# Gated mix of a long convolution and a mixer layer on one core: two row repairs of the filter fold done by VectorE, with another order of all instructions

## The chip, the cores and the metric

The kernel runs on one core of a Trainium2 chip. The metric is the device time of one execution in microseconds; shown are the median of several runs and one profiled execution. A core has five instruction queues that run side by side and meet only at semaphores: TensorE (PE, matmuls), VectorE (DVE), ScalarE (ACT), GpSimd (POOL) and SyncE (SP, which here only issues DMAs).

## The reference

The input x has 2048 rows of 640 bf16 values. Two branches are computed from it and mixed with a gate for each row.

```
g = sigmoid((x * gate_w).sum(-1))
a = x * (y + kv * ssm_D)        # kv = (k convolved with 4 taps) * v
                                # y  = long causal convolution of kv with ssm_k over 2048 rows, by FFT
h  = gelu(layernorm(x) @ w1)    # 640 -> 640, then its four quarters are shifted by 1, -1, 2, -2 rows
x1 = x + shifted(h) @ w2
b  = x1 + gelu(layernorm(x1) @ w3) @ w4     # 640 -> 1536 -> 640
out = g * a + (1 - g) * b
```

## The kernel before, in words

The rows form 16 tiles of 128 rows; the 640 channels form 5 chunks of 128.

**The mixer branch.** ln1 (L846) takes mean and variance of a tile with batch-norm instructions on VectorE, the reciprocal root (rstd) with one POOL instruction (L811), normalises on VectorE (L858) and transposes on TensorE (pe_turn, L839). mm1 (L863) multiplies by w1 and ScalarE applies gelu on the way out of PSUM. mm2 (L895) multiplies by w2 and adds the result to x on VectorE (L909, which also gives the row sums). ln2 (L916) normalises again: for tiles 0 to 7 on VectorE with a DMA transpose by SP (ln_apply, L825), for the others on ScalarE. mm3 (L930) and mm4 (L952) are the two large products, in four blocks of 512 rows.

**The convolution branch.** A transform of 2048 points is made of small matmuls with constant matrices, after rows have been added and subtracted in pairs ("folds") so that fewer products are needed. The filter's chunk c goes through three functions. h_load (L729) loads it. h_fold (L732) adds ssm_D, makes sums and differences of rows and their mirror on VectorE (L737, L738), copies the 16 unpaired elements (L739), and lets SP transpose the result into tile T (L740). A second fold (L721) then makes sums and differences of T into tile U. Two rows don't fit the pattern and are repaired on partition 0: in T a run of 4 x 128 elements is copied to another place of T (L743), and 8 x 128 elements of U overwrite elements of T (L744). h_chunk (L746) multiplies T and U with the constant Rh: its first four products read U (L749, L750), the other four read T (L751, L752) and so need the repairs. ScalarE copies each result out of PSUM into the filter's transform HF. The two pairs T, U alternate between chunks, so the fold of chunk c + 2 waits for the products of chunk c. The signal goes the same way: kv_load (L755) transposes k and v on loading, kv_fold (L762) makes the four taps, the product with v and the folds, x_fwd (L784) multiplies into XF. Later, unit (L972) multiplies the transforms on VectorE, with some sums made by accumulating DMAs from POOL (L987), and final (L1011) transforms back, applies the gate and either adds to the output in memory with an accumulating POOL DMA (L1036, for the first 12 of 16 units) or writes it by SP (L1039).

**What sets the order.** The program records 1200 operations in the order of the calls (L1054 to L1115). The list SEQUENCE holds their numbers in the order in which they are issued; each engine takes its own operations from that list, in order, and never overtakes. The numbers are those of recording, so number 410 is the same operation in any list. PLACES gives each of the 213 PSUM tiles its bank. schedule (L255) adds the dependence of a tile on the copying out of the tile that held its banks before, and emit (L276) turns the dependences that are left into semaphore waits. A DMA's place in the list is its place in the queue of its engine: the transfers of SP and the DMAs, rstd and gate instructions of POOL each wait in line.

Operations that the prediction names: 404, the second sum of the last filter fold (L724); 410, its first product on that sum (L750); 457, the normalising of tile 3 in ln2 (L826), whose transpose is 458; the first mm3 group (L934), which is 505 in the list before; 45, the load of Rh (L675); 349, h_load of chunk 2 (L730).

Of the kernel before, what the change touches and what calls it, by code (L numbers as in the profile page):

```python
# [414 lines left out]
def bass_gated_mix__ssm_conv_h3__mixer_s_mlp__prompt_kernel(  # L415
# [32 lines left out]
    def ps(n, cls):  # L448
# [3 lines left out]
    SEQUENCE = [40, 58, 0, 6, 2, 7, 5, 38, 41, 8, 59, 43, 3, 4, 1, 9, 39, 60, 10, 61, 11, 12, 46, 42, 13, 141, 14, 142, 15, 62,  # L452
# [463 lines left out]
    def ln2(t):  # L916
        ln_math(1, t)
        x, xn, mean, rstd = X[:, t, :], xnb[t % 3], st[1, 2][:, t:t + 1], st[1, 5][:, t:t + 1]
        if t < LNA:
            ln_apply(1, t, mean, x, xn, chunk_of[1, t // 4], ALU.add)  # L920
            return
# [226 lines left out]
```

## Time and profile before

| | |
|---|---|
| median of 3 runs | 234.4 us (234.22 to 234.96) |
| the profiled execution, whole | 233.44 us |
| its span, first to last instruction | 231.6 us |
| granted TensorE clock, mean | 0.990 |
| busy: PE, DVE, ACT, POOL | 215.5, 209.1, 187.2, 75.5 us |
| DMA packets, moved | 74258, 42.68 MB |

A line of the page's groups reads: line of the code, engine, operation, output and input with shape, count, then busy time, mean time of one in ns, and the idle time of the engine just before it with what ended it. "L615", "L620" and "L625" are the helpers through which nearly all VectorE and ScalarE instructions are recorded, "L635" the helper of the matmuls, "L238" of the DMAs. PSall is PSUM; arena is the one SBUF tensor that holds every tile. SPq and POOLq are DMA issues. Matmuls overlap in the records, so busy time divided by count is the better measure of what one costs.

### The profile page before, as it was taken

The numbers are of one execution on the slowest core, as the hardware profiler recorded it, in microseconds if no ns is written. First come the engines' busy times: TensorE is split into PE (matmuls) and PEld (weight loads), VectorE is DVE, ScalarE is ACT, GpSimd is POOL, SyncE is SP. The second block draws the span as 40 slices with busy tenths as digits, with TensorE's granted clock in tenths as the row PEclk, the third lists the DMA queues.
The fourth block names the chain that finished last, engine by engine and source line by source line (L and its number), as shares of the span: only waits on it lengthen the run. The fifth ranks groups of instructions, "written<-read, shape, count | busy, mean of one in ns | idle before, by whom it ended". The sixth has DMA issues, their size and how long they took to land.

```text
span 231.6 us, 3931 instructions
## 1 busy us (share of the span) xinstructions
PE 215.5 (93%) x1455; PEld 127.5 (55%) x1455; DVE 209.1 (90%) x362; ACT 187.2 (81%) x352; POOL 75.5 (33%) x86
## 2 busy tenths in 40 slices
PE   6989899999999987999999999999999999999940
PEld 2678555674554542445765456744677545777720
DVE  5997899998989969899969999998899999899890
ACT  2389979999999999999937999759998778436960
POOL 1313020244124030240344233442234352648851
PEclk9999999999999999999999999999999999999996
DMA  5999969997877997697798499699989999799994
GB/s 175 372 259 292 236 96 231 186 273 150 173 205 158 146 272 166 137 327 109 178 200 136 97 198 182 141 171 179 294 155 203 193 164 149 116 174 124 109 161 84
DMA packets 74258, 42.68 MB, mean 184 GB/s; under 512 B 54266, under 2 KB 69503, under 8 KB 74239
## 3 DMA queue, kind: packets, MB, share of 16 engines
q1 hardware_dynamic: 64912, 30.55, 55.1%
q0 software_dynamic: 9152, 11.82, 34.2%
q8 instruction: 11, 0.18, 0.3%
q10 hardware_dynamic: 174, 0.07, 0.2%
q14 instruction: 9, 0.07, 0.1%
HBM read 14.88 MB, written 6.55 MB: 93 GB/s over the span
## 4 chain that ended last, share of the span: by engine, by line
PE 64%; ACT 19%; DVE 6%; issue 3%; DMA 3%; POOL 2%; POOLq 1%
PE PSall L635 60%; ACT arena L625 19%; DVE arena L615 3%; PE PSall L658 3%; DMA arena<-arena 3%; POOL out_dram L238 2%; DVE arena L620 1%; PE PSall L841 1%; DVE arena L909 1%; POOLq L1118 1%; POOL arena L811 0%; DVE arena L655 0%; PE PSall L690 0%; DVE arena L645 0%; DVE arena L662 0%
## 5 line engine op out<-in xcount | busy, mean ns | idle before, releaser
L635 PE MATMUL PSall<-arena 128*128 128x320 bf16 (+4 forms) x1341 | 204.0, 310 | 5.9 <-ACT arena L625 3.4
L615 DVE TENSOR_TENSOR arena<-arena 128x320 bf16<-128x320 bf16 (+6 forms) x201 | 163.4, 862 | 6.7 <-ACT arena L625 3.1
L635 PEld LDWEIGHTS PSall<-arena 128*128 128x128 bf16 x1341 | 120.1, 98 | 88.9 <-ACT arena L625 14.5
L625 ACT ACTIVATE arena<-PSall 128x512 bf16<-128x512 f32 (+8 forms) x187 | 107.6, 626 | 19.0 <-PE PSall L635 13.7
L625 ACT ACTIVATE arena<-arena 128x1 f32<-128x1 f32 (+5 forms) x115 | 69.3, 645 | 6.6 <-POOL arena L811 3.4
L238 POOL DMA_DIRECT2D arena<-arena x22 | 20.5, 954 | 68.5 <-DVE arena L615 56.5
L238 POOL DMA_DIRECT2D out_dram<-arena x28 | 30.5, 1192 | 30.5 <-ACT arena L625 23.6
L811 POOL TENSOR_TENSOR arena<-arena 128x1 f32<-128x1 f32 (+1 forms) x26 | 23.0, 898 | 40.2 <-DVE arena L620 40.1
L625 ACT ACTIVATE arena<-PSall,arena 128x640 bf16<-128x640 f32 (+1 forms) x32 | 20.3, 657 | 10.0 <-PE PSall L635 9.4
L620 DVE TENSOR_SCALAR arena<-arena 128x640 bf16<-128x640 bf16 (+4 forms) x65 | 22.5, 367 | 3.1 <-ACT arena L625 2.2
L909 DVE SCALAR_TENSOR_TENSOR arena<-PSall,arena 128x640 bf16<-128x640 f32 x16 | 13.1, 820 | 4.3 <-PE PSall L635 4.1
L807 DVE BATCH_NORM_STATS2 arena<-arena 128x6 f32<-128x320 bf16 x32 | 14.2, 477 | 1.5 <-DMA arena<-in_A_q_dram 1.5
L658 PE MATMUL PSall<-arena 128*128 128x512 bf16 x28 | 8.4, 446 | 2.1 <-DVE arena L655 2.1
L841 PE MATMUL PSall<-arena 128*128 128x128 bf16 x80 | 6.7, 219 | 0.4 <-ACT arena L625 0.2
L658 PEld LDWEIGHTS PSall<-arena 128*128 128x128 bf16 x28 | 3.0, 112 | 5.6 <-DVE arena L655 2.1
L841 PEld LDWEIGHTS PSall<-arena 128*128 128x128 bf16 x80 | 5.0, 97 | 1.2 <-ACT arena L625 0.6
L620 POOL TENSOR_SCALAR arena<-arena 128x16 f32<-128x16 f32 x3 | 1.9, 635 | 10.8 <-ACT arena L625 10.0
L625 ACT ACTIVATION_READ_ACCUMULATOR arena<-arena 128x1 f32 x16 | 3.3, 208 | 0.0
L808 DVE BATCH_NORM_AGGREGATE arena<-arena 128x2 f32<-128x12 f32 x16 | 2.9, 197 | 0.1
L664 ACT ACT_TABLE_LOAD x1 | 1.3, 1283 | 2.1 <-issue 2.1
L615 POOL TENSOR_TENSOR arena<-arena 128x16 f32<-128x16 f32 x3 | 2.6, 869 | 0.7 <-DVE arena L620 0.5
L909 DVE DVE_READ_ACCUMULATOR arena<-PSall,arena 128x1 f32 x16 | 1.3, 82 | 0.0
(19 smaller groups left out, 3.4 us busy)
## 6 DMA issues: line engine op xcount, KB each, us to landing
arena<-arena POOLq DMA_DIRECT2D x12, 640.0 KB, 6.5
arena<-in_A_q_dram SPq DMA_DIRECT2D x14, 320.0 KB, 5.3
out_dram<-arena POOLq DMA_DIRECT2D x20, 160.0 KB, 4.4
arena<-in_A_ssm_k_dram SPq DMA_DIRECT2D x5, 512.0 KB, 4.7
arena<-in_B_w_dram SPq DMA_DIRECT2D x1, 1920.0 KB, 8.6
out_dram<-arena SPq DMA_DIRECT2D x10, 160.0 KB, 2.7
arena<-in_B_w_dram SPq DMA_DIRECT2D x1, 1152.0 KB, 5.5
out_dram<-arena SPq DMA_DIRECT2D x12, 80.0 KB, 2.7
```

Of the source, the lines that this page charges most:

```text
L238: fn = lambda e: e.dma_start(out, in_, **kw)
L615: P.op(eng, lambda e: e.tensor_tensor(o, real(a), real(b), op), [a, b], [o], dve_ns(o, [a, b], 2) if eng == "dve" else 500)
L620: P.op(eng, lambda e: e.tensor_scalar(o, real(a), s1, s2, op0=op0, **({} if op1 is None else {"op1": op1})), [a] + aps, [o], dve_ns(o, [a] ...
L625: P.op("act", lambda e: e.activation(real(o), real(a), f, bias=bias, scale=scale, **({"accum_out": accum} if accum is not None else {})), ...
L635: fns.append(lambda e, l=l, r=r, i=i: e.matmul(real(o), l, r, start=(i == 0), stop=(i == last)))
L658: P.op("pe", lambda e: e.matmul(real(pw), warm[:, 0:128], warm[:, 128:640], start=True, stop=True), [warm], [pw], 427.0)
L807: P.op("dve", lambda e, o=o, i=i: e.bn_stats(o, i), [i], [o], 400)
L808: P.op("dve", lambda e: e.bn_aggr(bna[:, t, :], bns[k]), [bns[k]], [bna[:, t, :]], 120)
L811: P.op("pool", lambda g: g.tensor_tensor(o, a, e, ALU.pow), [a, e], [o], dur)
L841: P.op("pe", [lambda e, c=c, pb=pb, xn=xn: e.transpose(real(pb)[:, 128 * c:128 * (c + 1)], xn[:, 128 * c:128 * (c + 1)], ident) for c in r ...
L909: P.op("dve", lambda e: e.scalar_tensor_tensor(x, real(pr), 1.0, x, op0=ALU.mult, op1=ALU.add, accum_out=st[1, 0][:, t:t + 1]), [pr, x], [ ...
L1118: with nc.Block() as block:
```

## The change

The two repairs of each chunk's fold, ten in all, are made by a VectorE tensor_scalar (times 1.0) on one partition instead of POOL DMAs. SEQUENCE and PLACES are new throughout: each operation keeps its number, the ten repairs move from POOL's queue to VectorE's, and the order on all five engines and the banks of most PSUM tiles are others. A branch in ln2 is added that PT2 = () leaves unused.

```
-    SEQUENCE = [40, 58, 0, 6, 2, 7, 5, 38, 41, 8, 59, 43, 3, 4, 1, 9, 39, 60, 10, 61, 11, 12, 46, 42, 13, 141, 14, 142, 15, 62,
...
+    SEQUENCE = [40, 58, 3, 1, 38, 8, 41, 59, 7, 6, 5, 9, 42, 4, 2, 0, 39, 60, 10, 11, 61, 12, 46, 13, 43, 141, 14, 15, 142, 16,
...
-    PLACES = [0, 1, 4, 2, 5, 0, 0, 1, 2, 3, 4, 5, 3, 2, 5, 6, 3, 5, 7, 3, 3, 0, 5, 4, 6, 1, 7, 0, 6, 3, 7, 3, 4, 4, 2, 3, 2, 2,
...
+    PLACES = [0, 1, 1, 2, 6, 5, 3, 2, 3, 4, 5, 6, 7, 6, 7, 1, 4, 1, 0, 7, 5, 1, 6, 6, 3, 2, 0, 5, 5, 2, 4, 5, 0, 7, 6, 0, 6, 6,
...
-        P.dma("pool", T5[0:1, :, 1, 1], T5[0:1, :, 0, 0])
-        P.dma("pool", T[0:1].rearrange("p (i e n) -> p i e n", e=2, n=128)[:, :, 0], U[0:1].rearrange("p (i e n) -> p i e n", e=2, n=128)[:, :, 1])
+        for o, a in ((T5[0:1, :, 1, 1], T5[0:1, :, 0, 0]),
+                     (T[0:1].rearrange("p (i e n) -> p i e n", e=2, n=128)[:, :, 0], U[0:1].rearrange("p (i e n) -> p i e n", e=2, n=128)[:, :, 1])):
+            if ROWFIX:
+                ts(o, a, 1.0, None, ALU.mult)
+            else:
+                P.dma("pool", o, a)
...
+    ROWFIX = 1
...
+        if t < LNA and t in PT2:
+            ts(xn, x, mean, rstd, ALU.add, ALU.mult)
+            pe_turn(t, xn, chunk_of[1, t // 4])
+            return
```

Where the places that the prediction names stand in the two lists (the numbers of the operations left and right of a mark; "..." leaves out what lies between):

```
before: ... 403 678 ... 404 ... 614 ... 753 ... 602 ... 410 411 ... 413 ... 505
after:  ... 404 ... 403 410 411 ... 405 ... 406 ... 753 ... 413 ... 457 ... 602 ... 511
before, SP: 202 (x), 327 (h_load 1), ... 349 (h_load 2), 310 (transpose, fold 0), 526 (v), 45 (Rh), 552 (k, chunk 1)
after,  SP: 202, 327, 305, ... 310, 552, 526, 349, 251 (x), 45
```

In the new list the first mm3 group is 511; between 410 and it stand three mm2 tiles (731, 732, 676, 677, 753, 754) and the products of chunk 4 and of x_fwd chunk 2.

138 rows, old and new, of tables (PLACES, SEQUENCE) are left out of this document.

## The prediction

> **What bounds the kernel now.** I read first the page's busy shares, then the windows by stage, then the timelines and the chain of waits in the one stage where TensorE stands still.
>
> ```profile
> span 231.6 us, 3931 instructions
> PE 215.5 (93%) x1455; PEld 127.5 (55%) x1455; DVE 209.1 (90%) x362; ACT 187.2 (81%) x352; POOL 75.5 (33%) x86
> ...
> 10.00:30.00 20.00, 18.07 (x223) 14.40 (x222) 18.00 (x56) 18.22 (x45) 3.61 (x5) 1.00 1.08 258
> 50.00:80.00 30.00, 29.07 (x206) 15.69 (x204) 28.27 (x57) 29.86 (x61) 7.62 (x10) 1.00 0.83 174
> 80.00:90.00 10.00, 7.89 (x42) 3.71 (x41) 7.74 (x15) 10.00 (x11) 2.27 (x4) 1.00 1.03 262
> 90.00:100.00 10.00, 9.75 (x46) 4.16 (x45) 9.11 (x12) 9.97 (x20) 1.47 (x2) 1.00 0.64 158
> 100.00:220.00 120.00, 120.00 (x750) 72.57 (x749) 113.55 (x136) 94.62 (x177) 49.07 (x47) 1.00 0.91 169
> ```
>
> The columns behind the stretch are its length, then PE, PEld, DVE, ACT and POOL busy, and the clock. From 100 to 220 us TensorE is busy 120.00 of 120.00 us at clock 1.00: nothing that feeds it there is worth anything unless it becomes late. What is to be had lies before. The idle time of PE is 1.93 us from 10 to 30, 0.93 from 50 to 80, and 2.11 + 0.25 = 2.36 from 80 to 100: 5.2 us at most. The stretch from 80 to 92 is where the last chunk of the filter fold and its repairs stand. VectorE is nearly as full as TensorE (28.27 of 30 us from 50 to 80), and the change gives it more to do.
>
> ```profile
> 75.66 6.59 PE L635 MATMUL PSall<-arena 128*128 128x512 bf16 x37
> 83.17 3.69 PE L635 MATMUL PSall<-arena 128*128 128x320 bf16 x20 [0.93 <-DVE arena L909]
> 87.88 1.04 PE L635 MATMUL PSall<-arena 128*128 128x512 bf16 x4 [1.01 <-ACT arena L625]
> 89.08 1.89 PE L635 MATMUL PSall<-arena 128*128 128x512 bf16 x8 [0.17 <-DMA arena<-arena]
> 91.22 1.04 PE L635 MATMUL PSall<-arena 128*128 128x512 bf16 x4 [0.25 <-ACT arena L625]
> ```
> ```profile
> 82.64 6.30 DMA arena<-arena
> ```
>
> The chain of waits (start, length, what) runs through the second repair of chunk 4: issued at 82.64, landed at 88.94, and the products that need it start at 89.08. But the timeline of PE beside it shows that the landing itself costs 0.17 us. The waits ahead of it are for L909 on VectorE (0.93) and for PSUM banks that ScalarE had not copied out (1.01 and 0.25). So a faster repair alone gives 0.17 us; the rest must come from the order.
>
> **The change, part by part.**
>
> *Ten transfers go.* Ten POOL DMAs (L743, L744) leave POOL and the queue.
>
> ```profile
> L238 POOL DMA_DIRECT2D arena<-arena x22 | 20.5, 954 | 68.5 <-DVE arena L615 56.5 <-DMA arena<-arena 12.0
> arena<-arena POOLq DMA_DIRECT2D x5, 1.0 KB, 2.3
> arena<-arena POOLq DMA_DIRECT2D x5, 2.0 KB, 3.4
> ```
>
> At 954 ns a DMA, POOL loses 9.5 us of 75.5 us busy; it is busy 33% of the span, so this is worth nothing by itself. What matters is POOL's queue: it stood 56.5 us behind the folds' VectorE instructions (L615), with rstd for later tiles queued behind. In the new order rstd and gate come right after each other. No row shows that a TensorE group waited for rstd, so I count nothing. The latency of 2.3 and 3.4 us goes from all five chunks; only chunk 4's is on the path (0.17 us).
>
> *Ten copies come to VectorE*, on one partition, 512 and 1024 elements. The trace has no copy on one partition of this length. The nearest rows:
>
> ```profile
> L679 DVE TENSOR_SCALAR arena<-arena 128x640 bf16<-128x640 bf16 x1 | 0.3, 272 | 0.0
> L620 DVE TENSOR_SCALAR arena<-arena 128x2048 bf16<-128x2048 bf16 x10 | 7.5, 745 | 0.1
> L620 DVE TENSOR_SCALAR arena<-arena 128x16 bf16<-128x16 bf16 x5 | 1.0, 202 | 0.1
> L655 DVE MEMSET arena<- 128x640 bf16 x1 | 0.6, 592 | 0.1
> ```
>
> The line through 640 elements (272 ns) and 2048 (745 ns) has 0.336 ns an element: 229 and 401 ns, five of each 3.15 us. From below, ten at the 202 ns of the 16-element form: 2.0 us. From above, the memset's 592/640 = 0.925 ns an element: 474 and 947 ns, 7.1 us. I take 3.15, since L679 is the same operation on the same type at nearly this length. The Trainium skill, "VectorE: DVE Perf Modes", section "The TRN2 errata", gives 58 cycles plus elements/4 at 0.96 GHz whatever the partitions; an estimate by that page is 194 and 327 ns, 2.6 us for the ten. The 272 ns row is above that page's 227 ns, so the row goes into the sum.
>
> *The new order at the end of the head.* The numbers of SEQUENCE are operations in the order of recording, so the two lists can be lined up. Three steps matter.
>
> First, chunk 4's products on U (op 410, L750), which started at 87.88. Of the work ahead of it on PE, three mm2 tiles (30 matmuls of 320 columns) and fourteen matmuls of 512 columns now stand behind it.
>
> ```profile
> L635 PE MATMUL PSall<-arena 128*128 128x320 bf16 x696 | 100.3, 299 | 3.2 <-ACT arena L625 1.2 <-DVE arena L615 1.1 <-DVE arena L909 0.9
> L635 PE MATMUL PSall<-arena 128*128 128x512 bf16 x420 | 96.1, 379 | 1.6 <-ACT arena L625 1.3 <-DMA arena<-arena 0.2
> 79.70 0.68 DVE L615 TENSOR_TENSOR arena<-arena 128x1024 bf16<-128x1024 bf16 x1
> 82.28 0.82 DVE L909 SCALAR_TENSOR_TENSOR arena<-PSall,arena 128x640 bf16<-128x640 f32 x1 [0.99 <-PE PSall L635]
> 83.03 0.44 DVE L620 TENSOR_SCALAR arena<-arena 128x640 bf16<-128x640 bf16 x1
> 84.74 0.82 DVE L909 SCALAR_TENSOR_TENSOR arena<-PSall,arena 128x640 bf16<-128x640 f32 x1 [1.27 <-PE PSall L635]
> ```
>
> Busy over count is 0.144 and 0.229 us, so PE has 30 x 0.144 + 14 x 0.229 = 7.5 us less to do first. It would be there at 87.88 - 1.01 - 0.93 - 7.5 = 78.4. It needs the fold's second sum (op 404), which ended at 79.70 + 0.68 = 80.4. Ahead of that, VectorE now has eight of the copies (4 x 0.63 = 2.5 us) and one small instruction (0.2), and no longer has one 1024-element sum, two L909, one 640-element and one small instruction (0.68 + 1.64 + 0.44 + 0.2 = 3.0): it ends 0.3 us sooner, at 80.1. So PE now waits 1.7 us there, for VectorE instead of ScalarE and the DMA. The two waits of VectorE for PE (0.99 and 1.27) should shrink, as the products that it waited for now come ahead of the instructions that read them.
>
> Second, the entry into mm3, from which PE does not stop again. Between op 410 and the first mm3 group lie 30 matmuls of 320 and 22 of 512 columns, 4.3 + 5.0 = 9.4 us: it starts at 80.1 + 9.4 = 89.5. Before, it started at 91.22 with four 512-column matmuls (0.9 us) more behind it, which is 90.3 in the new count. Gain 0.8 us. The condition is that tile 3's normalised rows have arrived.
>
> ```profile
> 76.66 1.20 SPq L235 DMA_TRANSPOSE arena<-arena  x1
> arena<-arena SPq DMA_TRANSPOSE x26, 3.7
> ```
>
> They left VectorE (op 457) for this transfer at 76.6. Op 457 now has more VectorE work ahead: ten copies 3.15, five 1024-element sums 3.4, one 2048-element scaling 0.75, two L909 1.64 and three small ones 0.84 are 9.8 us, less the 0.07 us by which each of the 21 overlaps the next (82.28 + 0.82 against the next start at 83.03), 8.3 us. It ends at 84.9, and 3.7 us later, at 88.6, mm3 can start: 0.9 us to spare.
>
> Third, SyncE. The constant of the filter transform (op 45) goes behind a transposed load of 3.88 us and two plain loads, h_load 2 (op 349) behind the same.
>
> ```profile
> 25.49 0.58 SPq L238 DMA_DIRECT2D arena<-cRh  x1
> 26.11 3.88 SPq L235 DMA_TRANSPOSE arena<-in_A_k_dram  x1
> 34.67 3.55 PE L635 MATMUL PSall<-arena 128*128 128x512 bf16 x15
> arena<-cRh SPq DMA_DIRECT2D x1, 448.0 KB, 4.6
> arena<-in_A_ssm_k_dram SPq DMA_DIRECT2D x5, 512.0 KB, 4.7
> ```
>
> The constant is issued at about 25.49 + 3.88 + 1.0 = 30.4 and lands at 35.0; its first product starts ten 512-column matmuls into the group at 34.67, near 36.8. Cost nothing, cover 1.8 us. h_load 2 leaves near 29.3 and lands at 34.0, for a VectorE instruction at 34.5: cover 0.5 us, and beyond it each microsecond is VectorE's and then PE's.
>
> *Other moves.* The 0.25 us at 91.22 was a bank: fewer banks are behind in the new list, since the chunk 4 copies-out stand earlier on ScalarE. I count 0.2. The rest of the banks and the moves on the first 30 us: same instructions, bound by the same loads; nothing, with 0.5 us either way. From 100 us on: nothing, while PE stays fed.
>
> *The end.* The last POOL write closes the span.
>
> ```profile
> 223.59 0.31 PE L635 MATMUL PSall<-arena 128*128 128x320 bf16 x1 [0.44 <-DVE arena L615]
> 225.29 1.20 POOL L238 DMA_DIRECT2D out_dram<-arena  x1 [2.54 <-DVE arena L615]
> ```
>
> Its unit's products (final 8, L1024) now have eight more matmuls behind them (1.2 us). But its own sums on VectorE now stand behind those of two more units, whose copies out come first on ScalarE; at 0.3 to 0.5 us for each such step I find some 1.2 us lost again. Nothing, 0.6 us either way.
>
> Sum: 0.8 + 0.2 + 0.2 = 1.2 us off a profiled execution of 231.6 us span (233.44 us in all). The median of the three runs is 234.4, 1.0 us above that execution; I take the same 1.2 off it: **233.2 us**.
>
> **The rivals.**
>
> *VectorE becomes the bound (slower).* Place: op 404, then every later wait of PE for it. Speaks for it: VectorE busy 28.27 of 30 us and 113.55 of 120 in the windows. If its idle 0.99 + 1.27 = 2.26 us is all that can take up the copies, the price is 3.15 - 2.26 = +0.9 us, 235.3, and with the upper 7.1 us +4.8, 239.2. It decides from the point at which the copies and the re-ordered sums end op 404 later than 80.1 + 1.2 = 81.3. Against it: 3.0 us of other work was moved behind. There is a second mechanism by which the copies could cost this much, a port that VectorE shares with POOL. DVE's L679 ran in 272 ns wholly inside a POOL instruction:
>
> ```profile
> 10.96 0.27 DVE L679 TENSOR_SCALAR arena<-arena 128x640 bf16<-128x640 bf16 x1
> 10.65 0.68 POOL L811 TENSOR_TENSOR arena<-arena 128x1 f32<-128x1 f32 x1 [2.35 <-DVE arena L620]
> ```
>
> If a copy instead had to wait out a POOL instruction, each of the ten would pay up to 0.7 us, +7 less the 2.26: +4.7, 239.1. As the row shows no such wait, I keep 0.02 of this rival's chance for it. The Trainium skill, "SBUF — State Buffer", section "Who interferes with whom", has such a rule, an exclusive lock between VectorE's copies in a two-port mode and GpSimd. These two rows disagree with it.
>
> *No change.* A late h_load 2 (1.2 us over its 0.5 us cover), or the end going the bad way, eats the gain: 234.4.
>
> *More than forecast.* The 0.94 us of PE idle time from 50 to 80 goes as well, and the 1.7 us wait at op 410 shrinks by the 1 us that VectorE loses waiting before it: -3.1, 231.3.
>
> *The change doesn't do what it says* would be copies far slower than 0.947 us, or split: the first rival's far end.
>
> **How the numbers follow.** Forecast 0.37, more 0.15, no change 0.18, VectorE bound 0.30 (0.02 of it the port). About 0.3% (0.7 us) is what a measurement can tell: faster 0.37 + 0.15 = 0.52, same 0.18, slower 0.30. The range runs from 231.2 (the greater gain) to 236.8, which leaves out the slower rival's dearer copies, about 0.1, and less than 0.1 below.
>
> **What would show it.** Ten copies of 0.2 to 0.45 us at L620; PE idle near 80 us released by L615 on DVE for about 1.7 us, and mm3 starting near 89.5; PE's 120 us from there unbroken; DVE idle between 80 and 90 under 1 us. I am wrong if PE shows new waits for DVE after 100 us, if the copies take 0.5 to 0.9 us, or if PE stands still near 35 us for a load.

## The result, and the profile after

The changed kernel takes 232.94 us (median of 19 runs, 231.40 to 234.95), the kernel before beside it 234.56 us (19 runs, 233.83 to 236.55). The ratio is 0.9929 with a 95% interval of 0.9906 to 0.9951: 1.6 us or 0.7% faster. Forecast were 233.2 us and a gain of 1.2 us. The profiled execution took 232.63 us in all. So the number came out; the experiments show that its terms did not.

First the page of the changed kernel with the shares of busy time, then its windows (length, then PE, PEld, DVE, ACT and POOL busy, and the clock; the last two numbers, on the DMA engines, are not used here):

```profile
span 230.8 us, 3937 instructions
...
PE 216.5 (94%) x1455; PEld 127.2 (55%) x1455; DVE 210.8 (91%) x372; ACT 185.7 (80%) x352; POOL 73.1 (32%) x76
```
```profile
10.00:30.00 20.00, 17.05 (x205) 13.02 (x202) 16.74 (x53) 17.10 (x42) 3.58 (x5) 1.00 1.09 264
50.00:80.00 30.00, 29.32 (x201) 15.47 (x201) 28.45 (x58) 29.88 (x60) 7.60 (x7) 1.00 0.76 162
80.00:90.00 10.00, 9.35 (x55) 4.93 (x52) 8.57 (x21) 10.00 (x13) 1.06 (x2) 1.00 1.13 233
90.00:100.00 10.00, 9.78 (x47) 4.24 (x46) 8.63 (x14) 10.00 (x22) 3.18 (x4) 1.00 0.98 276
100.00:220.00 120.00, 120.00 (x747) 71.98 (x746) 115.50 (x134) 94.42 (x178) 48.45 (x46) 1.00 0.87 161
```

Read beside the same rows of before: from 80 to 90 us PE is busy 9.35 us instead of 7.89, as was hoped. But from 10 to 30 us it is busy 17.05 instead of 18.07: 1.0 us is lost before 1.5 are gained.

The timeline of PE around the entry into mm3, and the groups of VectorE by form, where the ten copies stand:

```profile
75.73 4.67 PE L635 MATMUL PSall<-arena 128*128 128x512 bf16 x24
80.77 0.61 PE L635 MATMUL PSall<-arena 128*128 128x512 bf16 x2 [0.38 <-DVE arena L615]
81.66 8.57 PE L635 MATMUL PSall<-arena 128*128 128x320 bf16 x50 [0.28 <-ACT arena L625]
90.44 2.75 PE L635 MATMUL PSall<-arena 128*128 128x512 bf16 x12 [0.22 <-issue]
```
```profile
L620 DVE TENSOR_SCALAR arena<-arena 1x1024 bf16<-1x1024 bf16 x5 | 2.0, 407 | 0.0
L620 DVE TENSOR_SCALAR arena<-arena 1x512 bf16<-1x512 bf16 x5 | 1.4, 279 | 0.0
```

Op 410 starts at 80.77 behind a wait of 0.38 us for VectorE; the waits of 1.01 us for ScalarE and of 0.17 us for the landing are gone. mm3 starts at 90.44. The prediction put the entry of the kernel before, with the same work behind it, at 90.3. So at this place, in these two executions, the changed kernel stands where the other stood: the local gain has been paid with an equal loss ahead of it. The 0.8 us by which its span is shorter (230.8 against 231.6) show up only at the very end. Its last matmul and its last POOL write:

```profile
224.05 0.31 PE L635 MATMUL PSall<-arena 128*128 128x320 bf16 x1 [0.29 <-DVE arena L615]
225.17 1.21 POOL L238 DMA_DIRECT2D out_dram<-arena  x1 [0.89 <-DVE arena L615]
```

In the kernel before they begin at 223.59 and 225.29. So TensorE ends 0.5 us later than before, the last write is issued 0.1 us sooner, and the span ends 5.6 us behind the start of that write instead of 6.3.

### The profile page after: what moved, and what is told of

Its sections match the earlier page's. It is cut to its first block, busy times and chain, and to the rows that moved or that the text cites. A ratio compares the mean times of both kernels' runs of the same rounds, so it can differ in the third digit from the quotient of the medians.

```text
span 230.8 us, 3937 instructions
## 1 busy us (share of the span) xinstructions
PE 216.5 (94%) x1455; PEld 127.2 (55%) x1455; DVE 210.8 (91%) x372; ACT 185.7 (80%) x352; POOL 73.1 (32%) x76
## 4 chain that ended last, share of the span: by engine, by line
PE 69%; ACT 26%; DVE 2%; issue 1%; DVEq 0%; ACTq 0%
PE PSall L635 65%; ACT arena L625 26%; PE PSall L658 3%; DVE arena L615 1%; PE PSall L846 1%; DVE arena L655 0%; DVEq L1127 0%; PE PSall L690 0%; DVE arena L646 0%; DVE arena L648 0%; ACTq L364 0%; DVE arena L662 0%
## 5 line engine op out<-in xcount | busy, mean ns | idle before, releaser
L635 PE MATMUL PSall<-arena 128*128 128x320 bf16 (+4 forms) x1341 | 204.2, 310 | 4.6 <-ACT arena L625 2.2
L635 PEld LDWEIGHTS PSall<-arena 128*128 128x128 bf16 x1341 | 119.8, 98 | 87.4 <-ACT arena L625 13.6
L615 DVE TENSOR_TENSOR arena<-arena 128x2560 bf16<-128x2560 bf16 (+7 forms) x201 | 162.8, 861 | 4.9 <-ACT arena L625 2.0
L625 ACT ACTIVATE arena<-PSall 128x512 bf16<-128x512 f32 (+9 forms) x187 | 107.5, 636 | 19.4 <-PE PSall L635 11.1
L816 POOL TENSOR_TENSOR arena<-arena 128x1 f32<-128x1 f32 (+1 forms) x26 | 24.1, 954 | 71.5 <-DVE arena L620 71.4
L238 POOL DMA_DIRECT2D out_dram<-arena x28 | 31.3, 1241 | 37.9 <-ACT arena L625 32.9
L620 DVE TENSOR_SCALAR arena<-arena 128x640 bf16<-128x640 bf16 (+6 forms) x75 | 24.8, 361 | 3.9 <-ACT arena L625 2.8
L238 POOL DMA_DIRECT2D arena<-arena x12 | 16.6, 1384 | 29.9 <-DVE arena L615 29.9
L658 PE MATMUL PSall<-arena 128*128 128x512 bf16 x28 | 9.7, 478 | 1.8 <-DVE arena L655 1.8
L620 POOL TENSOR_SCALAR arena<-arena 128x16 f32<-128x16 f32 x3 | 2.6, 856 | 11.3 <-ACT arena L625 11.3
L615 POOL TENSOR_TENSOR arena<-arena 128x16 f32<-128x16 f32 x3 | 4.2, 1391 | 2.4 <-DVE arena L620 2.2
```

The costliest lines, as they stand in the source:

```text
L238: fn = lambda e: e.dma_start(out, in_, **kw)
L615: P.op(eng, lambda e: e.tensor_tensor(o, real(a), real(b), op), [a, b], [o], dve_ns(o, [a, b], 2) if eng == "dve" else 500)
L620: P.op(eng, lambda e: e.tensor_scalar(o, real(a), s1, s2, op0=op0, **({} if op1 is None else {"op1": op1})), [a] + aps, [o], dve_ns(o, [a] ...
L625: P.op("act", lambda e: e.activation(real(o), real(a), f, bias=bias, scale=scale, **({"accum_out": accum} if accum is not None else {})), ...
L635: fns.append(lambda e, l=l, r=r, i=i: e.matmul(real(o), l, r, start=(i == 0), stop=(i == last)))
L658: P.op("pe", lambda e: e.matmul(real(pw), warm[:, 0:128], warm[:, 128:640], start=True, stop=True), [warm], [pw], 427.0)
```

## The experiments

Every kernel has the code of the changed one; only the lists, the flag ROWFIX or what a diff shows differs. In the kernels whose matmul helper reads L643 instead of L635, the lines from the lists on stand 8 further down. "Old" is the order of the kernel before, "new" that of the changed kernel. Half a per cent is in question, so the control comes first.

### Control: the kernel before as a kernel under test

> The kernel before, unchanged, as a kernel under test: for a second profile and as a control of the comparison. If the comparison favours neither side, 234.4 to 235.0 and a ratio with 1 inside its interval. Theory H: the first profiled execution of the kernel before (233.44 us) was one of its fastest, by a head that happened to be short; this one stands at 35 us by TensorE work 0 to 1 us behind it, and is the same behind that. If the ratio comes out at 0.994 to 0.996 here too, the gain of the copies in the old order (0.9941, 0.9952) is none of the copies'.

Measured: 234.68 us (12 runs), ratio 0.9993 (0.9972 to 1.0014). The comparison favours neither side. Theory H fails as to the place: this profiled execution was 0.4 us longer than the first (span 232.0), but not in the head. The timeline of PE, and the step of the chain of waits ahead of it:

```profile
87.83 1.04 PE L635 MATMUL PSall<-arena 128*128 128x512 bf16 x4 [1.01 <-ACT arena L625]
89.39 1.89 PE L635 MATMUL PSall<-arena 128*128 128x512 bf16 x8 [0.53 <-DMA arena<-arena]
```
```profile
82.60 6.66 DMA arena<-arena
```

The repair took 6.66 us to land instead of 6.30, PE waited 0.53 instead of 0.17, and the last matmul began at 223.91 instead of 223.59. The transfer of one row of 2 KB stands directly on the path: in these two executions, what it lost (0.36 us), the kernel lost.

### The copies alone, in the old order (run twice)

```
-    SEQUENCE = [40, 58, 3, 1, 38, 8, 41, 59, 7, 6, 5, 9, 42, 4, 2, 0, 39, 60, ...
+    SEQUENCE = [40, 58, 0, 6, 2, 7, 5, 38, 41, 8, 59, 43, 3, 4, 1, 9, 39, 60, ...
```

(SEQUENCE and PLACES of the kernel before; ROWFIX = 1.)

> The kernel before with its own order and banks; only the ten repairs are made by VectorE instead of POOL DMAs. Theory 1, the copies are neutral by themselves: VectorE's 3.4 us go into its idle time, the 0.17 us behind the landing goes, 234.2 to 234.9, within 0.2% of the kernel before. Theory 2, the order needs the copies but the copies don't need the order: the same, 234.2 to 234.9. Rival 3, VectorE is the bound: its 2.26 us of idle time from 80 to 90 take up only a part, +0.9 us or more, 235.3 to 237.5. Rival 4, the removal of POOL's queue wait is the gain: 232.5 to 233.5.

> The old order with the copies on VectorE once more, to make its ratio (0.9941, 0.9916 to 0.9965) firmer. In its profile TensorE was at most 0.2 us better than before behind the head, and the end (last matmul to end of span) 0.35 us shorter. Theory 1, the copies alone are worth what the profile shows, 0.2 to 0.6 us: 234.0 to 234.4, ratio 0.997 to 0.999. Rival 4, they are worth 1 us: 233.5 to 233.8, ratio 0.993 to 0.996.

Measured: 233.75 us, ratio 0.9941 (0.9916 to 0.9965), and 233.59 us, ratio 0.9952 (0.9928 to 0.9976). The copies alone are worth 1.1 to 1.3 us by the medians (234.81 and 234.89 beside them), most of the whole change; the intervals overlap with that of the changed kernel (0.9906 to 0.9951). That the copies are neutral (theories 1 and 2 of the first run) and the rival of a full VectorE are out. The 0.2 to 0.6 us of the second run's theory 1 (0.997 to 0.999) lie outside the first interval and at the edge of the second. Rival 4, that the gain is that of the removed transfers, is nearest. The timeline of PE in the second run:

```profile
88.00 2.85 PE L635 MATMUL PSall<-arena 128*128 128x512 bf16 x12 [1.02 <-ACT arena L625]
91.42 1.89 PE L635 MATMUL PSall<-arena 128*128 128x512 bf16 x8 [0.57 <-ACT arena L625]
```

The four products of chunk 4 on T now follow the others without a break (twelve matmuls instead of four and eight). The bank wait behind them is 0.57 us instead of 0.25 (in the first run 0.34), so part of what the landing held up is now held up by ScalarE. The profiles thus show 0.2 to 0.4 us less here against the second profile of before, and nothing against the first. The rest of the span shows 0.3 to 0.4 us more: from the start of the last matmul to the end it is 231.3 - 223.59 = 7.7 us here, and 8.0 and 8.1 in the two profiles of before. Some 0.5 us of the 1.2 us is not seen in these profiles. Both profiled executions of before (233.44 and 233.83 us) were faster than its median; longer landings in the slower executions would explain the rest, but no trace of such an execution exists, so this stays open.

### The new order without the copies

```
-    ROWFIX = 1
+    ROWFIX = 0
```

> The changed kernel with the ten copies back as POOL DMAs, at their places in the new list; order and banks are the new ones. The times are against 234.5 us for the kernel before and 232.9 for the changed one. Theory 1, the order alone makes the gain and the copies are neutral: chunk 4's products on T (op 413, which started at 85.06 in the changed kernel) are late by at most 0.2 us, 232.7 to 233.2. Theory 2, the order needs the copies: the second repair of chunk 4 is issued at about 82.2 and lands 6.3 us later, as before, at 88.5, so TensorE stands up to 3 us in front of op 413; part of it overlaps the 0.2 us wait and the DVE-free time, so 1.5 to 3 us longer than the changed kernel, 234.4 to 236. Rival 3, VectorE is full and the copies cost their 3.4 us in part: this kernel is faster than the changed one, 230.5 to 232.5.

Measured: 250.25 us, ratio 1.0659 (1.0622 to 1.0696). Theory 2 is right in kind and far too small in size. The timelines of PE and POOL, and the windows of the two stretches:

```profile
58.95 7.32 PE L643 MATMUL PSall<-arena 128*128 128x512 bf16 x23 [4.48 <-DMA arena<-arena]
...
98.47 7.84 PE L643 MATMUL PSall<-arena 128*128 128x512 bf16 x30 [4.50 <-DMA arena<-arena]
```
```profile
69.09 1.54 POOL L824 TENSOR_TENSOR arena<-arena 128x1 f32<-128x1 f32 x2 [8.64 <-DVE arena L628]
...
90.29 0.57 POOL L238 DMA_DIRECT2D arena<-arena  x1 [3.48 <-DVE arena L623]
94.37 0.52 POOL L238 DMA_DIRECT2D arena<-arena  x1 [3.51 <-DMA arena<-arena]
```
```profile
50.00:65.00 15.00, 10.08 (x81) 5.41 (x80) 10.45 (x21) 8.09 (x24) 2.80 (x5) 0.77 0.56 123
90.00:105.00 15.00, 10.15 (x51) 5.30 (x51) 8.15 (x17) 9.35 (x11) 2.18 (x4) 0.89 0.97 225
```

Two things had been left out. The second repair writes the tile that the first has written, so POOL waits for the first to land (3.51 us) before it issues the second: by POOL a repair is two transfers one behind the other, from 90.29 to 98.47, or 8.2 us; by VectorE it is 0.279 + 0.407 = 0.69 us. And it happens again in earlier chunks: PE stands 4.48 us near 59 as well. The new order starts the products on T some 2 us behind the copies (82.84 and 85.06 for ops 406 and 413 in the changed kernel), so it cannot do without them. A third loss came on top. The clock, the third number from the end of each window, fell from 1.00 to 0.77 and 0.89 over 15 us; by an estimate from these figures that is 15 x 0.23 = 3.5 and 15 x 0.11 = 1.7 us of TensorE's time beside the two waits, together some 14 of the 17.3 us by which this kernel is slower than the changed one.

### Heads and rests exchanged

The first 288 operations stand as in the one list (up to about 39 us), all others in the order of the other; PLACES go with them. The seams, against the changed kernel and against the old order:

```
-                ... 351, 537, 698, 269, 317, 333, 321, 322, 270, 554, 699, 44, ...
+                ... 537, 699, 453, 320, 333, 252, 579, 351, 269, 321, 322, 270, 554, ...
```
```
-                ... 537, 699, 453, 320, 333, 324, 700, 687, 554, 335, ...
+                ... 269, 317, 333, 321, 322, 423, 454, 44, 334, 699, 453, 324, 700, ...
```

> The first 288 operations in the order and banks of the kernel before (up to about 39 us), all others in the new order; copies by VectorE. Comparing the profiles by TensorE work done, the changed kernel stands 1.85 us behind the kernel before at 35 us and makes it good between 80 and 90. Theory 1, that loss is the order's: with the old head all engines reach 39 us some 1.5 us earlier and the rest follows, 230.8 to 231.9, the fastest of all. Rival A, the loss is repaid by slack: VectorE's second fold of chunk 4 (op 404), which ended at 80.71, is bound by VectorE's own work, TensorE would wait there instead for up to 1.7 us: 232.5 to 233.2, as the changed kernel. Rival B, the loss lay in loads that happened to be slow in one execution: as the changed kernel, and its profile shows no loss at 35 us.

> The first 288 operations in the new order and banks, all others in the order of the kernel before; copies by VectorE, as in the changed kernel. Theory 1, the new head loses some 1.7 us and nothing behind it gives them back: 235.6 to 236.6. Rival A, the old rest is bound between 80 and 92 by VectorE and the repair chain, whatever TensorE had done before: part of the loss is hidden by the 2.1 us that TensorE stands there, 234.5 to 235.4. Rival B, the loss was an accident of one execution: 234.0 to 234.8.

Measured: old head with new rest 234.83 us, ratio 0.9988 (0.9961 to 1.0015); new head with old rest 234.77 us, ratio 0.9991 (0.9971 to 1.0011). Windows from 0 to 40 and from 75 to 100 us, of the old order with copies, the new head with the old rest, the old head with the new rest, and the changed kernel, in this order:

```profile
0.00:40.00 40.00, 35.96 (x311) 22.74 (x312) 34.18 (x102) 27.77 (x62) 5.73 (x12) 1.00 0.96 235
75.00:100.00 25.00, 22.70 (x113) 10.31 (x112) 22.82 (x39) 25.00 (x37) 3.55 (x7) 1.00 0.81 178
```
```profile
0.00:40.00 40.00, 34.98 (x309) 22.26 (x310) 34.20 (x102) 27.32 (x61) 5.69 (x12) 1.00 0.96 234
75.00:100.00 25.00, 22.70 (x114) 10.30 (x112) 22.83 (x39) 25.00 (x36) 3.82 (x7) 1.00 0.82 177
```
```profile
0.00:40.00 40.00, 36.16 (x311) 22.74 (x312) 34.14 (x101) 27.72 (x62) 5.72 (x12) 1.00 0.96 233
75.00:100.00 25.00, 24.34 (x125) 11.48 (x124) 22.17 (x40) 25.00 (x44) 5.96 (x7) 1.00 0.99 236
```
```profile
0.00:40.00 40.00, 35.00 (x306) 22.01 (x307) 33.90 (x102) 26.89 (x60) 5.68 (x12) 1.00 0.89 232
75.00:100.00 25.00, 24.09 (x125) 11.65 (x125) 22.21 (x42) 25.00 (x45) 5.71 (x7) 1.00 1.02 233
```

The two terms go with their lists: the new head costs PE 1.0 to 1.2 us of busy time (34.98 and 35.00 against 35.96 and 36.16), the new order from 75 to 100 us returns 1.4 to 1.6. That settles rival B: the loss in the head is the order's. (In the other profiles PE is busy 33.33 to 34.57 us up to 40 us with the new head, and 35.80 to 35.99 with the old head and the copies.) And the new head with the old rest is 1.0 to 1.2 us slower than the old order with copies, as much as its head loses. But the old head with the new rest, which should have been fastest, was not. Its timelines of POOL, VectorE, ScalarE and PE near 145 us:

```profile
141.80 3.83 POOL L824 TENSOR_TENSOR arena<-arena 128x1 f32<-128x1 f32 x2
```
```profile
141.74 2.96 DVE L623 TENSOR_TENSOR arena<-arena 128x2560 bf16<-128x2560 bf16 x3
```
```profile
145.15 1.70 ACT L633 ACTIVATE arena<-arena 128x1 f32<-128x1 f32 x4 [3.55 <-POOL arena L824]
```
```profile
147.81 1.80 PE L643 MATMUL PSall<-arena 128*128 128x320 bf16 x12 [0.80 <-ACT arena L633]
150.71 11.65 PE L643 MATMUL PSall<-arena 128*128 128x512 bf16 x58 [1.09 <-ACT arena L633]
```

An rstd of one column on POOL (op 716), which takes 0.56 us in the changed kernel, takes 3.32; ScalarE waits 3.55 us for it, and PE stands for 1.9 us. This happened after 100 us, in a stretch that the prediction counted at nothing.

### A race of 0.1 us between POOL and VectorE

In the changed kernel the same place looks like this, POOL first, then VectorE:

```profile
140.98 1.93 POOL L816 TENSOR_TENSOR arena<-arena 128x1 f32<-128x1 f32 x2
```
```profile
141.01 9.51 DVE L615 TENSOR_TENSOR arena<-arena 128x2560 bf16<-128x2560 bf16 x8
```

There POOL began 0.03 us before VectorE's product 824, and op 716, the first of the two instructions of this row, took 0.56 us. With the old head it began 0.06 us behind. Four kernels test whether this order decides. The first exchanges two small instructions of VectorE ahead of 824:

```
-                813, 864, 723, 715, 716, 654, 726, 824, 865, ...
+                813, 864, 723, 654, 726, 715, 716, 824, 865, ...
```

> The changed kernel with two small instructions of VectorE exchanged: 726 (tile 12, 0.2 us) now comes ahead of 715 (tile 11, 0.2 us), and the rstd of tile 11 on POOL (op 716), which waits for 715, is so released just after the 2560-element product 824 begins and not just before it. Nothing else. Seen so far: op 716 took 0.56 us in the changed kernel, where it began 0.03 us before 824, and 3.32 us with the old head, where it began 0.05 us after 824 and ended 0.42 us after the third of three long VectorE instructions. Theory L, a POOL instruction that comes second is held until VectorE leaves a gap: 716 takes 2.5 to 3.4 us, ScalarE's normalising of tile 11 comes 2 to 3.5 us later, TensorE stands some 2.4 us near 150, 234.5 to 235.6. Rival R, POOL's long spans are only how the profile draws them, and the stall with the old head came from the order around it: no change from the changed kernel, 232.5 to 233.3.

Measured: 234.75 us (233.25 to 237.80), ratio 0.9995 (0.9964 to 1.0025) against 0.9929: 1.5 us more than the changed kernel by the ratios and 1.8 by the medians, so nearly the whole gain, from the exchange of two instructions of 0.2 us. POOL, VectorE and ScalarE:

```profile
143.68 3.71 POOL L816 TENSOR_TENSOR arena<-arena 128x1 f32<-128x1 f32 x2 [0.25 <-DVE arena L620]
```
```profile
143.50 2.95 DVE L615 TENSOR_TENSOR arena<-arena 128x2560 bf16<-128x2560 bf16 x3
```
```profile
146.91 1.70 ACT L625 ACTIVATE arena<-arena 128x1 f32<-128x1 f32 x4 [3.63 <-POOL arena L816]
```

VectorE's three instructions end at 146.45 and ScalarE is released at 146.91: POOL got its turn only when VectorE left a gap. The profiled execution (236.58 us) was one of the slowest, and it was late before the exchange could act: product 824 begins at 143.50 instead of 141.01. Of the 4.0 us by which its span is longer than the changed kernel's, 2.5 therefore lie ahead of the exchange, and 1.5 behind it. The next two put POOL's DMA 813 behind the rstd, with the new and with the old head:

```
-                813, 864, 723, 715, 716, 654, 726, 824, 865, ...
+                864, 723, 715, 716, 813, 654, 726, 824, 865, ...
```

> The changed kernel with one operation of POOL moved: the accumulating DMA 813 of a unit comes behind the rstd of tile 11 (716) instead of ahead of it, so that 716 is always released by VectorE's small 715 and begins before the long product 824. Theory L: 716 takes 0.5 to 0.6 us in every execution, the executions of the changed kernel above 234 us (4 of 19) go, 813 is 0.6 us later and has room; median 232.3 to 232.9. Rival R: no change of the median or of the spread, 232.7 to 233.2, and if 813 is what the next VectorE sums wait for, up to 0.6 us slower.

> The old head (first 288 operations) with the new rest, as in the run before, and op 813 behind 716 on POOL. With the old head alone TensorE was 0.3 us ahead of the changed kernel at 140 us and then stood for 2.4 us. Theory L: 716 takes 0.5 to 0.6 us, the 2.4 us go, 232.0 to 232.7, the fastest so far. Rival R: the stall stays, 234.3 to 235.2.

Measured: 238.87 us, ratio 1.0152 (1.0109 to 1.0195), and 237.38 us, ratio 1.0110 (1.0070 to 1.0149). Both expectations missed. The rstd still came second: with the old head it began at 141.08 and took 3.33 us, beside three products of VectorE from 141.03 on, and 813 was now held up behind it (issued at 144.37 instead of near 140). The move didn't do what it was meant to and added a wait: PE stands 3.38 us ahead of 152.28 with the old head and 3.52 us ahead of 153.24 with the new one, for a reason that the profile doesn't name ("issue"). Part of the loss is the clock, which is below 1.00 in the windows of these two profiles, old head first:

```profile
140.00:160.00 20.00, 15.99 (x92) 9.28 (x92) 15.85 (x18) 11.64 (x24) 9.33 (x9) 0.91 0.76 154
140.00:160.00 20.00, 16.48 (x95) 9.99 (x94) 16.50 (x18) 11.02 (x23) 7.47 (x6) 0.83 0.77 146
```

In the changed kernel, and in the kernels of this section with shorter waits, it is 1.00 there. The fourth kernel leaves POOL alone and lets VectorE come 0.25 us later, with the old head:

```
-                813, 864, 723, 715, 716, 654, 726, 824, 865, ...
+                813, 864, 723, 715, 716, 654, 726, 1200, 1201, 824, 865, ...
...
+    for _ in range(2):
+        ts(st[0, 3][:, 0:1], st[0, 3][:, 0:1], 1.0, None, ALU.mult)
```

> The old head (first 288 operations) with the new rest, and two VectorE instructions more on one dead column (128x1, some 0.25 us together) between 726 and the long product 824, so that the rstd of tile 11 on POOL (716) begins before 824 in every execution. Nothing is moved on POOL. With the old head alone 716 came 0.05 us behind 824, took 3.32 us, and the median was 234.83; the move of a POOL DMA lost that race as well (3.33 us). Theory L, POOL is held when it comes second: 716 takes 0.5 to 0.7 us, TensorE's 2.4 us of standing near 150 go, 232.0 to 232.7, faster than the changed kernel by up to 0.9. Rival R, the stall comes from the order of ScalarE around it: 716 short, but TensorE still stands near 150, 234.3 to 235.2.

Measured: 233.14 us (231.56 to 233.78), ratio 0.9913 (0.9881 to 0.9946), 1.7 us less than the same kernel without the two instructions (234.83). POOL and VectorE:

```profile
142.05 2.08 POOL L816 TENSOR_TENSOR arena<-arena 128x1 f32<-128x1 f32 x2
```
```profile
142.25 8.09 DVE L615 TENSOR_TENSOR arena<-arena 128x2560 bf16<-128x2560 bf16 x7
```

POOL comes first again, its two rstd take 2.08 us instead of 3.83, and VectorE runs on. Theory L holds, from both sides: in the three profiles in which 716 began 0.03 to 0.26 us ahead of 824 it took 0.56 us (the third is that of the next section), and in the four in which it began 0.05 to 0.18 us behind it took 3.20 to 3.33. In the profile of this kernel PE waited 0.87 us near 149 for another transfer, so not all of the expected gain was seen.

The Trainium skill, "SBUF — State Buffer", section "Who interferes with whom", states this rule: a VectorE instruction with two SBUF inputs contends with a GpSimd instruction that reads SBUF, the second comer is blocked, and "Issue order, not op shape, decides who blocks". These runs agree: 0.56 us when POOL came first, 3.2 to 3.3 when second.

### Second copies

Each copy is made a second time, into a free place:

```
-                ts(o, a, 1.0, None, ALU.mult)
+                z = AR[0:1, oUT + 4096:oUT + 4096 + n_of(a)].rearrange("p (i n) -> p i n", n=128)
+                P.op("dve", [lambda e, o=o, a=a: e.tensor_scalar(o, a, 1.0, None, op0=ALU.mult),
+                             lambda e, z=z, a=a: e.tensor_scalar(z, a, 1.0, None, op0=ALU.mult)], [a], [o, z], 600)
```

> The kernel of the run above, and each of the ten copies has a second one behind it that writes the same values to a free place: 3.4 us more on VectorE, all before 84 us. Rival V, VectorE is the bound in the folds: the eight second copies ahead of op 404 push it back by most of 2.7 us, TensorE stands longer in front of op 410 (0.38 us in the changed kernel), and the time is 2 to 3.5 us above the run above. Theory O, the folds have room: VectorE's waits (some 1.5 us between 50 and 80, 1.4 between 80 and 90) take them up, 0 to 1 us above the run above.

Measured: 232.68 us, ratio 0.9916 (0.9887 to 0.9944): the same as with single copies. The window and the timeline of PE:

```profile
50.00:80.00 30.00, 29.23 (x193) 14.83 (x189) 30.00 (x63) 29.88 (x56) 7.91 (x6) 1.00 0.84 179
```
```profile
79.64 0.60 PE L635 MATMUL PSall<-arena 128*128 128x512 bf16 x2 [0.47 <-DVE arena L615]
```

VectorE is now busy 30.00 of 30 us, and PE still waits only 0.47 us in front of op 410. Rival V is out: in the folds there is room for twice the copies.

### The new tail

The first 1052 places of the list are the old order's (to about 197 us), the rest stand in the new order; copies by VectorE. The seam against the old order:

```
-                ... 942, 1049, 935, 1015, 1087, 1017, 943, 1088, 1062, 972, 1018, 1050, ...
+                ... 942, 1049, 935, 1015, 1087, 1017, 943, 1062, 1050, 1088, 966, 1089, ...
```

> The old order with the copies on VectorE (median 233.59 and 233.75 in two runs) up to about 197 us (1052 operations), and the new order behind it: only the last 30 us change. In the profiles the stretch from TensorE's last matmul to the end of the span is 7.4 to 7.7 us in the old order and 6.4 to 6.7 in the new one. Theory E, the new tail ends the program sooner, some 0.8 us less: 232.6 to 233.1. Rival F, TensorE ends as much later as the stretch is shorter, so that the tail is neutral: 233.4 to 234.0.

Measured: 233.20 us, ratio 0.9931 (0.9909 to 0.9953), between the two expectations and within the intervals of the old order with copies. The last matmul, here and in the first run of the old order with copies (span 232.0):

```profile
span 231.6 us, 3927 instructions
```
```profile
224.69 0.31 PE L635 MATMUL PSall<-arena 128*128 128x320 bf16 x1 [0.28 <-DVE arena L615]
```
```profile
224.34 0.31 PE L643 MATMUL PSall<-arena 128*128 128x320 bf16 x1 [0.44 <-DVE arena L623]
```

The stretch behind it is 231.6 - 224.69 = 6.9 us instead of 7.7, but PE ends 0.35 us later. Both happen; 0.4 us remain in the profiles, and the times can't tell that from nothing.

## Why the prediction was right, and where it was wrong

The number was right, partly by luck: terms missed in both directions, and the sum counts 0.4 us twice. The 90.3 us of the old entry into mm3 already have the two waits in them, 0.17 us for the landing and 0.25 us for the bank, while the 89.5 of the new one leave both out. So the gain of 0.8 us contains the 0.2 and 0.2 that the sum adds again; by its own steps the forecast would have been 233.6 us.

Of the signs that the prediction named, the copies' length (0.28 and 0.41 us) and the unbroken 120 us of PE came. The wait of 1.7 us near 80, mm3 at 89.5 and an idle time of VectorE under 1 us between 80 and 90 (it is 10 - 8.57 = 1.43 us) did not.

*The copies' duration*: forecast 229 and 401 ns, 3.15 us; measured 279 and 407 ns, 3.4 us. The Trainium skill, "VectorE: DVE Perf Modes", section "The TRN2 errata", gave 2.6 us by its formula; the same section says that the formula under-predicts and that the fixed part measured is about 150 cycles, which is an estimate of 290 and 423 ns. The measured values lie near that.

*What the transfers cost (forecast 0.17 us)*: this is the step that failed most. "So a faster repair alone gives 0.17 us" was read from one execution. A second has 0.53, and the copies alone bring 1.1 to 1.3 us by the medians, of which the profiles show about half. Some 0.3 us of that half lies behind the last matmul, where the prediction counted nothing for the transfers; where the other half lies stays open.

*The order at op 410*: VectorE's part came 0.6 us late, PE's 2.0 us. Op 410 starts at 80.77 (80.1 forecast), mm3 at 90.44 (89.5). The wait in front of op 410 was not 1.7 us but 0.38, because PE itself got there at 75.73 + 4.67 = 80.40 and not at the 78.4 of the sum. About half of these 2.0 us is the head's loss, an estimate from the profiles with the new rest: with the old head PE gets there at 79.2, 79.3, 80.1 and 80.5 us, with the new one at 80.4, 80.9 and 81.2. The bank wait of 0.25 us counted as gone has a like one in its place (0.28 at 81.66).

*The first 30 us*: "same instructions, bound by the same loads; nothing, with 0.5 us either way". Measured: 1.0 to 1.2 us lost. So in PE's busy time most of the 1.4 to 1.6 us gained from 75 to 100 is cancelled, and the forecast 0.8 is not the reason for the result. The times confirm the loss with the old rest alone (1.0 to 1.2 us). With the new rest, and the race out of the way, the old head should have been some 1 us faster than the changed kernel; by the ratios (0.9913 and 0.9916 against 0.9929) it was 0.3 us, well inside the intervals. What takes up the rest there is not shown. The loads that it feared (Rh, h_load 2) were not late: the changed kernel's PE has no wait for a DMA from 31 to 40 us. It lost before that, in waits of 0.84, 0.81 and 0.55 us for ScalarE:

```profile
22.51 1.53 PE L635 MATMUL PSall<-arena 128*128 128x320 bf16 x10 [0.84 <-ACT arena L625]
...
26.91 0.45 PE L846 MATMUL PSall<-arena 128*128 128x128 bf16 x5 [0.81 <-ACT arena L625]
...
30.28 0.85 PE L635 MATMUL PSall<-arena 128*128 128x320 bf16 x5 [0.55 <-ACT arena L625]
```

From 10 to 31 us its waits for ScalarE are 2.78 us in all (with 0.58 at 11.99). In the kernel before they are 1.59, and behind 20 us one of 0.68 us (at 24.52) is the only one: its list has 80 small matmuls in one piece ahead of it (7.18 us from 16.66 on), the new list 65 (from 16.99 to 21.67). Which of the moves in the head costs the time was not isolated.

*The end*: forecast nothing, 0.6 either way. From the start of the last matmul to the end it is 8.0 us in the kernel before and 230.8 - 224.05 = 6.75 in the changed one, 1.3 us less, which more than covers the 0.8 us of the span. Of this, 0.3 us came with the copies in the old order; the rest is the new tail's, which by itself let PE end 0.35 us later, so that 0.4 us of it remained.

*From 100 us on*: forecast nothing while PE stays fed. True in the profiled execution, but by 0.03 us: the rstd of tile 11 could have come second. Four of the 19 runs lie above 234.1, 0.6 us from the next, which would fit a lost race; that is only argued.

*The rivals*: the full VectorE fell (twice the copies cost nothing). The second mechanism, the shared port, was put aside with a row in which VectorE was not held up. What the runs show is another pair with the roles reversed: VectorE's products of two SBUF operands hold up POOL's rstd. No run shows a copy held up; they took 279 and 407 ns. "No change" fell. The greater gain did not come.

No kernel here is clearly faster than the changed one: the old head with the filler (0.9913) and with second copies (0.9916) overlap with 0.9929.

## What to carry to other kernels

A small transfer on the path is to be priced from its spread over executions and with every transfer that it must follow, not from the wait that one profile shows. A copy that an engine can make in 0.7 us on one partition is worth more than it seems, since it also lets an order be chosen that a transfer of 8 us would forbid. When a new order moves everything, count the stretch that seems unaffected too, by PE's busy time in the same windows: here PE lost there most of what the aimed-at stretch gained.

## What the runs showed of the hardware

- A POOL instruction on one column (op 716) took 0.56 us when it began 0.03 to 0.26 us before a chain of VectorE instructions on two SBUF operands, and 3.20 to 3.33 us when it began 0.05 to 0.18 us after it (seven profiles). In the second case it did not get its turn between the first and the second or the second and the third of them, which followed without a gap. The next rstd (717) of the changed kernel did: it began inside the first of them, at 141.51, and ended at 142.91, 1.40 us later, while VectorE went on. What makes the difference was not tested.
- Where TensorE stood still for 4.5 us (the new order without the copies), the granted clock of the 15 us around it was 0.77 and 0.89 instead of 1.00, so that standing still cost more than its own length. The same came after 3.38 and 3.52 us (the two kernels with 813 moved: 0.91 and 0.83 over 20 us), and not after the two shorter waits of 1.46 and 1.32 us in the kernel with 715 and 726 exchanged.
- A 2 KB transfer on POOL's queue, issued at the same point of the same kernel, landed after 6.30 us in one execution and after 6.66 in another, and the span grew by about the difference (0.4 us).
